# Convolution lags 0-15 by Karatsuba over pairs of token blocks, x and y in one buffer, and one filter strip of three loaded whole

## The chip, the cores and the metric

The kernel runs on one core of one Trainium2 chip. The metric is the device time of a run in microseconds. The four runs of the kernel before lie within 0.3% (2352.9 to 2360.5 us). Where a kernel was timed in rounds against the kernel before, the text gives the median and the ratio with its 95% interval; the other experiments are single runs with a profile. Profiles come from the hardware profiler on that core.

## The reference, cut to what matters

A causal convolution along the sequence, one filter per channel, is followed by a mixing layer, which the change does not touch.

```
x: (8, 5696, 128) float32        # batch, tokens, channels
h: (5696, 128) float32
y = irfft(rfft(x, n=2*S, axis=1) * rfft(h, n=2*S, axis=0), n=2*S, axis=1)[:, :S, :]
out = mixing_layer(y)            # two 5696 x 5696 products and more, 1765 us of the kernel before
```

## The kernel before: the parts that matter

Tokens are cut into 45 blocks of 128. For a channel d and a lag of k blocks, the filter gives a 128 x 128 Toeplitz matrix (each of its diagonals holds one value), and the matmul of lag k multiplies it with the first 45 - k blocks of x (8 batches each), so it has 8 x (45 - k) columns. The 45 matmuls of a channel accumulate into half of a tile in PSUM, the memory that matmuls write; the copy of a finished result out of it is called its eviction.

A Toeplitz matrix for all lags is a "strip": partition p holds the padded filter from place p on. A strip of 15 lags is read from memory into 64 partitions only (each row starts 2 bytes later than the row before). The other 64 partitions need the same data 64 places on, and VectorE copies them. Which half is loaded, and from which queue, alternates.

```python
x_sb = xsb_pool.tile([P, D, NT, B], BF16)                  # x, channel outermost
y_sb = ysb_pool.tile([P, NT, B, D], BF16)
...
with tc.tile_pool(name="conv_sbuf", bufs=6) as csb, ... :
    for d in range(D):
        ...
        for k0 in range(0, NT, KS):                        # KS = 15: three strips per channel
            strip = csb.tile([P, KS * P + 64], BF16, tag="strip")
            n_ = d * 3 + k0 // KS
            own, other, c0, c1 = ((slice(0, 64), slice(64, P), 0, 64) if n_ % 2 == 0 else
                                  (slice(64, P), slice(0, 64), 64, 0))
            eng = nc.sync if n_ % 2 == 0 else nc.scalar
            eng.dma_start(strip[own, :w + 64], ...)        # [[1, 64], [1, w + 64]] of h_pad
            nc.vector.tensor_copy(strip[other, c0:c0 + w], strip[own, c1:c1 + w])      # L158
            for k in range(k0, k1):                                                   # L162
                nc.tensor.matmul(psum[:, B * k: B * k + B * ntj], strip[:, c:c + P],
                                 x_sb2[:, d, :B * ntj], start=(k == 0), stop=(k == NT - 1))
        if d % 2 == 1:
            nc.scalar.activation(y_sb[...], pair[...], AF.Copy)                        # L167
```

## Time and profile before

The median is 2358.3 us of 4 runs (2352.9 to 2360.5).

| stage of the profiled run (2352.5 us) | us |
|---|---|
| filter and x loads, until the first matmul of the convolution | 108.1 |
| convolution, L162 | 479.8 |
| mixing layer | 1764.7 |

The first line below is part 1 of the page of the kernel before: each engine's busy time, its share of the span, and its number of instructions.

```profile
PE 2191.6 (93%) x14686; PEld 1210.8 (51%) x14686; DVE 1650.1 (70%) x2997; ACT 462.6 (20%) x669; POOL 798.2 (34%) x1474
```

A share over the whole span mixes stages with different limits. The next lines are the windows view of the same kernel for three stretches inside the convolution. Each line has the stretch, its length, busy us and instructions of PE (TensorE), PEld (its weight loads), DVE (VectorE), ACT (ScalarE) and POOL, then the granted clock, the DMA engines' mean busy share and the GB/s they moved.

```profile
core 0: us, PE busy (x) PEld busy (x) DVE busy (x) ACT busy (x) POOL busy (x), PEclk, DMA share, GB/s
200.00:300.00 100.00, 98.75 (x1206) 84.66 (x1203) 53.19 (x82) 11.13 (x14) 0.00 (x0) 1.00 0.74 207
300.00:400.00 100.00, 98.25 (x1204) 83.80 (x1202) 51.66 (x80) 10.31 (x13) 0.00 (x0) 1.00 0.73 206
400.00:500.00 100.00, 98.86 (x1211) 84.32 (x1210) 53.34 (x82) 11.13 (x14) 0.00 (x0) 1.00 0.73 206
```

TensorE is busy for 98 to 99% of the stage, VectorE for half of it, ScalarE for a tenth, and the DMA engines are not full. So TensorE sets the time of this stage.

From the groups of the page before: line, engine, operation, out<-in, shapes and number; then busy us and mean ns of one; then the engine's idle time in front of them and what ended it.

```profile
L162 PE MATMUL pair<-x_sb,strip 128*128 128x360 bf16 (+44 forms) x5760 | 472.0, 243 | 8.9 <-DVE strip L158 7.0
L158 DVE COPY strip<-strip 64x1920 bf16<-64x1920 bf16 x384 | 251.5, 655 | 228.1 <-DMA strip<-h_pad 194.8
```

The mean of 243 ns is a matmul's latency, not its cost: matmuls overlap (5760 of 243 ns would be 1400 us, in a stage of 480). The cost is the distance from one start to the next, which is in the trace: 152 ns for 360 columns, 99 for 232, 79 for 184, 56 for 128, and 25 for 40 columns and fewer. A line fitted to these, N/2.4 + 2.4 ns, meets the trace's medians from 360 down to 72 columns within 1.1 ns; no distance is under 25.

From part 6 of the same page, the DMA issues of the strips: queue, number, KB each, and the median us from issue to landing.

```profile
strip<-h_pad SPq DMA_DIRECT2D x192, 248.0 KB, 4.3
strip<-h_pad ACTq DMA_DIRECT2D x192, 248.0 KB, 4.3
```

### The profile page before, as it was taken

What the parts mean: (1) busy time and instruction counts of PE and PEld (TensorE: products, weight loads), DVE (VectorE), ACT (ScalarE), POOL (GpSimd) and SP (SyncE); (2) the same over time, 40 slices, a digit from 0 to 9 for tenths busy, and PEclk for the clock granted to TensorE, in tenths of its full rate; (3) what the DMA queues carried; (4) which work ended last, traced back from release to release, by engine and by line L of the source; (5) the groups of instructions that cost most, each with busy time, mean ns of one, the idle gap of its engine ahead of it and who ended that gap; (6) DMA issues with size and microseconds to landing.
All of it is one profiled execution on the core that took longest, in us unless ns stands there. A gap on an engine that the chain in (4) does not pass through costs nothing.

```text
span 2352.5 us, 39824 instructions
## 1 busy us (share of the span) xinstructions
PE 2191.6 (93%) x14686; PEld 1210.8 (51%) x14686; DVE 1650.1 (70%) x2997; ACT 462.6 (20%) x669; POOL 798.2 (34%) x1474
## 2 busy tenths in 40 slices
PE   4699999999657999999999999799999999999997
PEld 1188888888433444444444444334444444444443
DVE  5655555555668888887787677787777677677674
ACT  3411111110842332332322000001111111111111
POOL 0000000000211554554446654344454444544540
PEclk8599999999978999999999999999999999999998
DMA  9977777776997988998789997967887877977872
GB/s 240 251 208 205 206 203 207 207 205 192 261 293 192 162 165 162 166 167 152 139 163 167 156 151 131 291 107 130 146 144 134 153 140 131 156 133 136 152 133 56
DMA packets 435330, 405.50 MB, mean 172 GB/s; under 512 B 66496, under 2 KB 370624, under 8 KB 435008
## 3 DMA queue, kind: packets, MB, share of 16 engines
q0 software_dynamic: 222816, 131.33, 42.8%
q1 hardware_dynamic: 193936, 211.78, 30.6%
q10 hardware_dynamic: 18384, 59.85, 8.7%
q8 instruction: 116, 1.90, 0.3%
q14 instruction: 78, 0.64, 0.1%
HBM read 449.27 MB, written 84.75 MB: 227 GB/s over the span
## 4 chain that ended last, share of the span: by engine, by line
PE 77%; DMA 13%; DVE 6%; issue 2%; ACT 1%; SPq 1%; POOL 1%; DVEq 0%; ACTq 0%; POOLq 0%
PE m L604 56%; PE pair L162 15%; DMA strip<-h_pad 4%; DMA tmp<-in_x_dram 2%; DMA wb<-in_moe_w_tok_r_dram 2%; DVE c L611 1%; DMA b<-zi_hbm 1%; DMA h_bf<-in_h_dram 1%; PE v L425 1%; PE utp L418 1%; PE m L566 1%; PE m L568 1%; PE m L608 1%; DMA wb<-in_moe_w_tok_i_dram 1%; DVE wt L341 1%
## 5 line engine op out<-in xcount | busy, mean ns | idle before, releaser
L332 POOL DMA_DIRECT2D wb<-in_moe_w_tok_i_dram x720 | 390.6, 555 | 796.4 <-DVE wt L341 709.9
L332 POOL DMA_DIRECT2D wb<-in_moe_w_tok_r_dram x720 | 389.2, 557 | 704.5 <-PE pair L162 584.1
L162 PE MATMUL pair<-x_sb,strip 128*128 128x360 bf16 (+44 forms) x5760 | 472.0, 243 | 8.9 <-DVE strip L158 7.0
L604 PE MATMUL m<-b,wt 128*128 128x512 bf16 x1936 | 454.8, 381 | 18.7 <-ACT red L224 8.0
L162 PEld LDWEIGHTS <-strip 128*128 128x128 bf16 x5760 | 404.0, 98 | 77.6 <-DVE strip L158 12.9
L341 DVE STREAM_TRANSPOSE wt<-wb 128x384 f32<-128x384 f32 (+2 forms) x720 | 359.2, 522 | 119.9 <-PE m L604 72.0
L158 DVE COPY strip<-strip 64x1920 bf16<-64x1920 bf16 x384 | 251.5, 655 | 228.1 <-DMA strip<-h_pad 194.8
L604 PEld LDWEIGHTS <-wt 128*128 128x128 bf16 x1936 | 190.0, 98 | 252.1 <-issue 23.5
L611 DVE TENSOR_TENSOR c<-c,m 128x512 f32<-128x512 f32 x440 | 283.0, 668 | 0.0
L420 ACT ACTIVATE uts<-utp 128x512 bf16<-128x512 bf16 (+1 forms) x90 | 53.3, 592 | 614.4 <-PE utp L418 614.4
L167 ACT ACTIVATE y_sb<-pair 128x720 bf16<-128x720 f32 x64 | 50.9, 795 | 429.8 <-PE pair L162 368.1
L415 ACT ACTIVATE ub<-c 128x512 bf16<-128x512 f32 (+1 forms) x90 | 56.5, 628 | 224.6 <-DVE c L611 224.4
L121 PE MATMUL rps<-tmpbf,R_bf 128*128 128x512 bf16 x90 | 46.2, 616 | 51.0 <-DVE tmpbf L118 50.8
L118 DVE CAST tmpbf<-tmp 128x1024 bf16<-128x1024 f32 x45 | 56.4, 1261 | 32.4 <-DMA tmp<-in_x_dram 32.2
L191 ACT ACTIVATE yT<-tpz 128x512 bf16<-128x512 bf16 x68 | 39.7, 596 | 191.3 <-PE tpz L187 149.6
L427 DVE SCALAR_TENSOR_TENSOR c<-v,c 128x512 f32<-128x512 f32 (+1 forms) x90 | 61.4, 682 | 10.9 <-PE v L425 10.4
L205 ACT ACTIVATE red<-theta_ps,magic 128x512 f32<-128x512 f32 x46 | 31.6, 687 | 150.9 <-PE theta_ps L203 127.5
L225 ACT ACTIVATE mag<-mag,half_pi 128x512 f32<-128x512 f32 (+1 forms) x68 | 57.8, 851 | 0.2
L123 ACT ACTIVATE x_sb<-rps 128x1024 bf16<-128x1024 f32 x45 | 46.1, 1024 | 57.5 <-PE rps L121 57.2
L611 DVE TENSOR_TENSOR c<-yy,m 128x512 f32<-128x512 bf16 x88 | 56.0, 677 | 0.9 <-PE m L604 0.9
L121 PEld LDWEIGHTS <-R_bf 128*128 128x128 bf16 x90 | 6.2, 111 | 88.9 <-DVE tmpbf L118 80.1
L223 ACT ACTIVATE mag<-red 128x512 f32<-128x512 f32 x46 | 29.0, 630 | 78.0 <-DVE red L207 78.0
(2759 smaller groups left out, 2977.3 us busy)
## 6 DMA issues: line engine op xcount, KB each, us to landing
strip<-h_pad SPq DMA_DIRECT2D x192, 248.0 KB, 4.3
strip<-h_pad ACTq DMA_DIRECT2D x192, 248.0 KB, 4.3
wb<-in_moe_w_tok_r_dram POOLq DMA_DIRECT2D x352, 96.0 KB, 4.4
wb<-in_moe_w_tok_i_dram POOLq DMA_DIRECT2D x352, 96.0 KB, 4.8
wb<-in_moe_w_tok_r_dram POOLq DMA_DIRECT2D x352, 80.0 KB, 4.5
wb<-in_moe_w_tok_i_dram POOLq DMA_DIRECT2D x352, 80.0 KB, 3.7
tmp<-in_x_dram SPq DMA_DIRECT2D x44, 512.0 KB, 5.8
cp_hbm<-c SPq DMA_DIRECT2D x88, 256.0 KB, 2.4
```

Source lines behind the costliest of these rows:

```text
L118: nc.vector.tensor_copy(tmpbf, tmp.transpose([0, 2, 1]))
L121: nc.tensor.matmul(rps[:, h2 * 64:(h2 + 1) * 64, :], R_bf, tmpbf[:, h2 * 64:(h2 + 1) * 64, :], start=True, stop=True)
L158: nc.vector.tensor_copy(strip[other, c0:c0 + w], strip[own, c1:c1 + w])
L162: nc.tensor.matmul(psum[:, B * k: B * k + B * ntj], strip[:, c:c + P], x_sb2[:, d, :B * ntj], start=(k == 0), stop=(k == NT - 1))
L225: nc.scalar.activation(mag, mag, AF.Sin, bias=half_pi, scale=-TWO_PI)
L332: nc.gpsimd.dma_start(wb[32 * i:32 * i + 32, :ng, :nj * 64], bass.AP(tensor=a.tensor, offset=a.offset + row0 * S + p * H + i * QR + j0 * 6 ...
L341: nc.vector.transpose(wt.rearrange("p j t r -> p (j t r)").bitcast(F32).rearrange("p (j g t) -> p g j t", j=TJ, g=4)[:, :ng, :nj], wb[:, : ...
L415: nc.scalar.activation(ub[:m].rearrange("p b d -> p (b d)"), c[:m], AF.Copy)
L420: nc.scalar.activation(uts[:, :, :m], utp[:, :, :m], AF.Copy)
L427: nc.vector.scalar_tensor_tensor(c[:m], v[:m], 0.0, c[:m], op0=ALU.max, op1=ALU.add)
L604: nc.tensor.matmul(ms[q], a[q][:, j, :, r], bts[jj][q][:, r, :], start=(jj == 0 and r == 0), stop=(jj == NJ - 1 and r == 1 and q not in left))
L611: nc.vector.tensor_tensor(c, z, ms[q], op=op)
```

## The change

The intent is to take work from TensorE. Lags 0 to 15 couple token blocks in pairs (even and odd blocks), and three products of half length replace four (Karatsuba's scheme): the common term is taken once, from the difference of an even and an odd block of x, and the sums of neighbouring lags of the filter make the other two. That costs VectorE two sums and a difference per pair of channels, and an eviction with an addition in place of a plain copy. To pay for it, ScalarE takes over the copy of one strip, and the third strip is loaded into all 128 partitions, so that it needs no copy. x and y share one buffer, with channels innermost; each pair's x is copied out of it. All strips are issued from one queue (SyncE).

```diff
-    x_sb = xsb_pool.tile([P, D, NT, B], BF16)
+    xy = xy_pool.tile([P, NT + 1, B, D], BF16)
+    y_sb = xy[:, :NT, :, :]
...
+    LAGS = ((0, 2 * KX, 64), (2 * KX, 31, 64), (31, NT, 0))          # KX = 8
+    with tc.tile_pool(name="conv_strip", bufs=4) as csb, tc.tile_pool(name="conv_x", bufs=3) as cxb, ...
+        def conv_strips(d):
+            for n_, (k0, k1, halo) in enumerate(LAGS):
+                src = h_pad.offset + d * HW + P * k0
+                if halo == 0:                                         # the whole strip
+                    nc.sync.dma_start(strip, bass.AP(..., offset=src, ap=[[1, P], [1, w]]))
+                    continue
+                lower = (d + n_) % 2 == 0                             # own: 0-63 or 64-127
+                nc.sync.dma_start(strip[own, :], bass.AP(..., ap=[[1, 64], [1, w + 64]]))
+                if n_ == 0:
+                    nc.vector.tensor_copy(strip[other, ...], strip[own, ...])             # L156
+                else:
+                    nc.scalar.activation(strip[other, ...], strip[own, ...], AF.Copy)     # L158
+            nc.vector.tensor_add(q_, s0_[:, c0:c0 + w], s0_[:, c0 + P:c0 + P + w])        # L163
+        def conv_prepare(d):                                          # a pair of channels
+            nc.scalar.activation(xp..., xy[:, :, :, d:d + 2]..., AF.Copy)                 # L171
+            strips = [conv_strips(d + e) for e in range(2)]
+            nc.vector.tensor_sub(vd..., xp[:, :, 0, :, :]..., xp[:, :, 1, :, :]...)       # L175
+        nxt = conv_prepare(0)
+        for d in range(0, D, 2):
+            xp, vd, strips = nxt
+            nxt = conv_prepare(d + 2)                                 # one pair ahead
+            for e in range(2):
+                for k in range(KX):                                   # 24 products, L196-L200
+                    matmul(c_, b_, vd); matmul(odd blocks, q_, xp even); matmul(even blocks, q_, xp odd)
+                matmul(...)                                           # one of 120 columns, L203
+                for k in range(2 * KX, NT):                           # lags 16-44 as before, L209
+                    matmul(r, strip, xt)
+            nc.scalar.activation(c_sb..., c_ps..., AF.Copy)                               # L213
+            nc.vector.tensor_tensor(y of even blocks, rv[:, 0], cv, op=add)               # L217
+            nc.vector.tensor_tensor(y of odd blocks, rv[:, 1], cv, op=ALU.subtract)       # L218
```

More of the change, by code (lines that the diff above doesn't have):

```diff
@@ L40 @@
     HW = Sp + P
-    KS = 15
-    assert NT % KS == 0
     BD = B * D
@@ L74 @@
     ysb_ctx = ExitStack()
-    xsb_ctx = ExitStack()
-    xsb_pool = xsb_ctx.enter_context(tc.tile_pool(name="xsb", bufs=1))
-    x_sb = xsb_pool.tile([P, D, NT, B], BF16)
-    with tc.tile_pool(name="s0", bufs=1, side="right") as s0, \
-         tc.tile_pool(name="xload", bufs=4, side="right") as xl, \
+    xy_pool = ysb_ctx.enter_context(tc.tile_pool(name="xy", bufs=1, side="right"))
+    xy = xy_pool.tile([P, NT + 1, B, D], BF16)
+    y_sb = xy[:, :NT, :, :]
+    nc.vector.memset(xy[:, NT, :, :], 0.0)
+    with tc.tile_pool(name="s0", bufs=1) as s0, \
+         tc.tile_pool(name="xload", bufs=4) as xl, \
          tc.tile_pool(name="xlp", bufs=2, space=bass.MemoryType.PSUM) as xlp, \
@@ L116 @@
                                       ap=[[D, q_cnt], [S * D, B], [1, D]]))
-            tmpbf = xl.tile([P, D, B], BF16, tag="xbf")
-            nc.vector.tensor_copy(tmpbf, tmp.transpose([0, 2, 1]))
-            rps = xlp.tile([P, D, B], F32, tag="rps")
+            tmpbf = xl.tile([P, B * D], BF16, tag="xbf")
+            nc.vector.tensor_copy(tmpbf, tmp.rearrange("p b d -> p (b d)"))
+            rps = xlp.tile([P, B * D], F32, tag="rps")
             for h2 in range(2):
-                nc.tensor.matmul(rps[:, h2 * 64:(h2 + 1) * 64, :], R_bf,
-                                 tmpbf[:, h2 * 64:(h2 + 1) * 64, :], start=True, stop=True)
-            nc.scalar.activation(x_sb[:, :, tj, :], rps, AF.Copy)
+                nc.tensor.matmul(rps[:, h2 * 512:(h2 + 1) * 512], R_bf,
+                                 tmpbf[:, h2 * 512:(h2 + 1) * 512], start=True, stop=True)
+            nc.scalar.activation(xy[:, tj, :, :].rearrange("q b d -> q (b d)"), rps, AF.Copy)
         t = s0.tile([P, P], F32, tag="wt1")
@@ L130 @@
         nc.vector.tensor_copy(w_ch_sb, t)
-    ysb_pool = ysb_ctx.enter_context(tc.tile_pool(name="ysb", bufs=1, side="right"))
-    y_sb = ysb_pool.tile([P, NT, B, D], BF16)
-    x_sb2 = x_sb.rearrange("q d t b -> q d (t b)")
-    with tc.tile_pool(name="conv_sbuf", bufs=6) as csb, \
-         tc.tile_pool(name="conv_psum", bufs=2, space=bass.MemoryType.PSUM) as cps:
-        for d in range(D):
-            if d % 2 == 0:
-                pair = cps.tile([P, 2, 512], F32, tag="convps")
-            psum = pair[:, d % 2, :NT * B]
-            for k0 in range(0, NT, KS):
-                k1 = k0 + KS
-                w = KS * P
-                j0 = P * k0
-                strip = csb.tile([P, KS * P + 64], BF16, tag="strip")
-                n_ = d * 3 + k0 // KS
-                own, other, c0, c1 = ((slice(0, 64), slice(64, P), 0, 64) if n_ % 2 == 0 else
-                                      (slice(64, P), slice(0, 64), 64, 0))
-                eng = nc.sync if n_ % 2 == 0 else nc.scalar
-                eng.dma_start(strip[own, :w + 64],
-                              bass.AP(tensor=h_pad.tensor, offset=h_pad.offset + d * HW + j0,
-                                      ap=[[1, 64], [1, w + 64]]))
-                nc.vector.tensor_copy(strip[other, c0:c0 + w], strip[own, c1:c1 + w])
-                for k in range(k0, k1):
-                    ntj = NT - k
-                    c = c0 + (k - k0) * P
-                    nc.tensor.matmul(psum[:, B * k: B * k + B * ntj],
-                                     strip[:, c:c + P],
-                                     x_sb2[:, d, :B * ntj],
-                                     start=(k == 0), stop=(k == NT - 1))
-            if d % 2 == 1:
-                nc.scalar.activation(
-                    y_sb[:, :, :, d - 1:d + 1].rearrange("q t b e -> q (t b) e"),
-                    pair[:, :, :NT * B].rearrange("q e n -> q n e"), AF.Copy)
@@ L170 @@
-    xsb_ctx.close()
+    KX = 8
+    NJ2 = (NT + 1) // 2
+    assert NT == 2 * NJ2 - 1
+    LAGS = ((0, 2 * KX, 64), (2 * KX, 31, 64), (31, NT, 0))
+    with tc.tile_pool(name="conv_strip", bufs=4) as csb, \
+         tc.tile_pool(name="conv_x", bufs=3) as cxb, \
+         tc.tile_pool(name="conv_psum", bufs=2, space=bass.MemoryType.PSUM) as cps:
+        def conv_strips(d):
+            out_ = []
+            for n_, (k0, k1, halo) in enumerate(LAGS):
+                w = (k1 - k0) * P
+                strip = csb.tile([P, w + halo], BF16, tag=f"strip{n_}", name=f"strip{n_}")
+                src = h_pad.offset + d * HW + P * k0
+                if halo == 0:
+                    nc.sync.dma_start(strip, bass.AP(tensor=h_pad.tensor, offset=src,
+                                                     ap=[[1, P], [1, w]]))
+                    out_.append((strip, 0, k0))
+                    continue
+                lower = (d + n_) % 2 == 0
+                own, other, c0, c1 = ((slice(0, 64), slice(64, P), 0, 64) if lower else
+                                      (slice(64, P), slice(0, 64), 64, 0))
+                nc.sync.dma_start(strip[own, :],
+                                  bass.AP(tensor=h_pad.tensor, offset=src,
+                                          ap=[[1, 64], [1, w + 64]]))
+                if n_ == 0:
+                    nc.vector.tensor_copy(strip[other, c0:c0 + w], strip[own, c1:c1 + w])
+                else:
+                    nc.scalar.activation(strip[other, c0:c0 + w], strip[own, c1:c1 + w], AF.Copy)
+                out_.append((strip, c0, k0))
+            s0_, c0, _ = out_[0]
+            w = (2 * KX - 1) * P
+            q_ = csb.tile([P, w], BF16, tag="stripq", name="stripq")
+            nc.vector.tensor_add(q_, s0_[:, c0:c0 + w], s0_[:, c0 + P:c0 + P + w])
+            return out_, q_
+        def conv_prepare(d):
+            if d >= D:
+                return None
+            xp = cxb.tile([P, NJ2, 2, B, 2], BF16, tag="xp", name="xp")
+            nc.scalar.activation(xp.rearrange("q j p b e -> q (j p b) e"),
+                                 xy[:, :, :, d:d + 2].rearrange("q t b e -> q (t b) e"), AF.Copy)
+            strips = [conv_strips(d + e) for e in range(2)]
+            vd = cxb.tile([P, NJ2, B, 2], BF16, tag="vd", name="vd")
+            nc.vector.tensor_sub(vd.rearrange("q j b e -> q j (b e)"),
+                                 xp[:, :, 0, :, :].rearrange("q j b e -> q j (b e)"),
+                                 xp[:, :, 1, :, :].rearrange("q j b e -> q j (b e)"))
+            return xp, vd, strips
+        nxt = conv_prepare(0)
+        for d in range(0, D, 2):
+            xp, vd, strips = nxt
+            nxt = conv_prepare(d + 2)
+            r_ps = cps.tile([P, 2, 512], F32, tag="rps", name="r_ps")
+            c_ps = cps.tile([P, 2, 256], F32, tag="cps", name="c_ps")
+            for e in range(2):
+                (s0_, s1_, s2_), q_ = strips[e]
+                r = r_ps[:, e, :NT * B]
+                rj = r_ps[:, e, :2 * NJ2 * B].rearrange("q (j p b) -> q j p b", p=2, b=B)
+                c_ = c_ps[:, e, :NJ2 * B]
+                xt = xp.rearrange("q j p b e -> q (j p b) e")
+                strip, c0, _ = s0_
+                for k in range(KX):
+                    n = NJ2 - k
+                    b_ = strip[:, c0 + 2 * k * P:c0 + (2 * k + 1) * P]
+                    nc.tensor.matmul(c_[:, B * k:], b_, vd[:, :n, :, e],
+                                     start=(k == 0), stop=(k == KX - 1))
+                    nc.tensor.matmul(rj[:, k:NJ2 - 1, 1, :], q_[:, 2 * k * P:(2 * k + 1) * P],
+                                     xp[:, :n - 1, 0, :, e], start=(k == 0), stop=False)
+                    nc.tensor.matmul(rj[:, k:, 0, :],
+                                     q_[:, (2 * k - 1) * P:2 * k * P] if k else b_,
+                                     xp[:, :n, 1, :, e], start=False, stop=False)
+                nc.tensor.matmul(rj[:, KX:, 0, :], strip[:, c0 + (2 * KX - 1) * P:c0 + 2 * KX * P],
+                                 xp[:, :NJ2 - KX, 1, :, e], start=False, stop=False)
+                for strip, c0, k0 in (s1_, s2_):
+                    k1 = LAGS[1][1] if strip is s1_[0] else NT
+                    for k in range(k0, k1):
+                        c = c0 + (k - k0) * P
+                        nc.tensor.matmul(r[:, B * k:B * NT], strip[:, c:c + P],
+                                         xt[:, :B * (NT - k), e], start=False, stop=(k == NT - 1))
+            rv = r_ps[:, :, :2 * NJ2 * B].rearrange("q e (j p b) -> q p j b e", p=2, b=B)
+            c_sb = cxb.tile([P, NJ2, B, 2], F32, tag="csb", name="c_sb")
+            nc.scalar.activation(c_sb.rearrange("q j b e -> q (j b) e"),
+                                 c_ps[:, :, :NJ2 * B].rearrange("q e n -> q n e"), AF.Copy)
+            cv = c_sb
+            yv = xy[:, :, :, d:d + 2].rearrange("q (j p) b e -> q p j b e", p=2)
+            nc.vector.tensor_tensor(yv[:, 0], rv[:, 0], cv, op=add)
+            nc.vector.tensor_tensor(yv[:, 1, :NJ2 - 1], rv[:, 1, :NJ2 - 1], cv[:, :NJ2 - 1],
+                                    op=ALU.subtract)
```

## The prediction

> **What bounds the kernel now.** The change touches only the convolution. By line L162 its 5760 matmuls run from 108.1 to 587.7 us, 480 of 2352.5 us. TensorE bounds this stage: the windows 200-500 us show it 98 to 99% busy, VectorE 52%, ScalarE 11%, DMA share 0.73 at 206 GB/s. From the trace, one matmul follows the other after N/2.4 + 2.4 ns for N columns, never under 25 ns (360 columns 152 ns, 184 columns 79 ns, up to 40 columns 25 ns; strip boundaries excepted). A channel's 45 matmuls are then 3.62 us, 464 us for 128; the other 16 us are the half clock until 122.6 us and short waits for strips (20 us in the line view).
>
> **What changes on TensorE.** Lags 0-15 cost 4800 columns per channel, 2.04 us; Karatsuba does them with 24 half-length products and one of 120 columns, 3800 in all, so 1.64 us. Lags 16-44 stay at 1.59 us. That is 3.23 us per channel, 413 us for 128: 50 us less. This holds if strided operands (every second bf16; sums in runs of 8 floats) stream at the same rate; no matmul of this trace shows it.
>
> **What is added, per pair of channels (6.46 us of TensorE).** VectorE: two copies of half a strip (0.655 us for 1920 columns now, about 0.7 for 2048); two bf16 sums of 1920 columns (1024 take 0.68 us, 768 take 0.56, so 1.15 each); the difference, 0.4; two eviction sums of 368 and 352 floats (512 take 0.67, so 0.52): about 5.2 us. ScalarE: two half copies of 1920 (1024 elements take 1.02, so 1.8 each), the pair's x 0.83, the eviction 0.45: about 4.9 us. Both fit, VectorE at 80%, in a loop (eviction of a pair, then preparing the next but one) with little slack.
>
> DMA: a channel's strips grow from 762 to 983 KB because one is loaded whole, so 300 GB/s is wanted against 206. The page loads x at 287 and the products' operands at 360 GB/s; but half strips landing behind each other at the start came every 1.17 us, 217 GB/s. [...] If half strips do not overlap, 1.25 + 1.17 + about 1.15 = 3.6 us per channel, which would bind; overlapped, 3.0. I expect mostly overlap: 3.3 us.
>
> **Ends of the stage.** Strips can no longer be loaded during the x loads (their memory is what those loads use), and halves, sums and differences precede the first matmul: about +7 us. Last eviction +1. The x cast without transpose is cheaper, but x loading is bound by its DMA (tiles every 1.8 us): 0 to -2.
>
> **Sum.** 3.3 x 128 = 422, +7 half clock, +7 start, +1, a few us of waits: about 441 against 480. The rest is unchanged. Prediction **2321 us**, 2300 to 2352 eight times in ten. Faster by over 2% (under 2312) 0.34, within 2% 0.62, slower 0.04.
>
> **In the profile.** L162's successors: 54 matmuls per channel, 6912; stage about 440 us; same spacing per column; VectorE 75 to 85% there, ScalarE about 75%; DMA near 290 GB/s; first matmul near 114 us.
>
> **What would make it wrong.** Strided operands streaming slower; the strips' DMA binding at 3.6 us (then about 2355, TensorE waiting on strips); the VectorE loop longer than TensorE's 6.46 us; or less waiting than thought, which gives 2305.

422 + 7 + 7 + 1 and a few us of waits came to about 441 us for the stage, and 2321 in all. The 217 GB/s is the trace's (248 KB every 1.17 us); the 1.15 us of a whole strip and the 3.0 us of a channel with overlap were estimates, not shown by the trace (for the whole strip, the 377 GB/s of its window 1480 to 1485 us, a high one, would make it 1.22). The half clock until 122.6 us is not in the trace either: the granted clock is 0.50 from 108.1 to 112.0 us and 1.00 from there to 130.

## The result

The changed kernel takes 2432.4 us (median of 4 runs, 2427.8 to 2436.5) against 2358.3 us, both correct. The ratio is 1.032, with an interval of 1.029 to 1.035: slower by 3.2%. A ratio here is the mean time of one kernel's fast runs over that of the other's in the same rounds, so not quite the ratio of the medians quoted.

| stage of the profiled run | before | after |
|---|---|---|
| until the first matmul of the convolution | 108.1 | 111.0 |
| convolution | 479.8 | 549.3 |
| mixing layer | 1764.7 | 1765.7 |
| span | 2352.5 | 2426.1 |

The whole loss is in the convolution: 69.6 of 73.5 us, with 2.9 us more in front of it. Part 1 of the page after:

```profile
PE 2167.8 (89%) x15665; PEld 1237.5 (51%) x15838; DVE 1684.1 (69%) x3062; ACT 728.1 (30%) x861; POOL 796.7 (33%) x1474
```

The windows view after, same stretches and columns as before:

```profile
200.00:300.00 100.00, 82.74 (x1244) 77.73 (x1242) 54.74 (x79) 56.73 (x46) 0.00 (x0) 0.98 1.04 231
300.00:400.00 100.00, 84.22 (x1291) 78.93 (x1289) 58.07 (x84) 59.52 (x48) 0.00 (x0) 1.00 1.04 238
400.00:500.00 100.00, 84.17 (x1300) 80.73 (x1298) 58.07 (x84) 59.46 (x48) 0.00 (x0) 0.98 1.03 237
```

TensorE is no longer the limit (83 to 84%), and neither are VectorE and ScalarE (below 60%). The DMA engines' share has gone from 0.73 to 1.04, which is full: 231 to 238 GB/s. A channel's strips are 983,040 bytes (64 x 4224 + 64 x 3968 + 128 x 3584), so 4.15 us per channel at the 237 GB/s of the last window. 128 of them are 531 us of the stage's 549; from 120 to 200 us the rate was lower, 215 to 217 GB/s.

The strips' issues after, from part 6 of the page; the first line is the whole strips:

```profile
strip<-h_pad SPq DMA_DIRECT2D x128, 448.0 KB, 11.5
strip<-h_pad SPq DMA_DIRECT2D x128, 264.0 KB, 11.4
strip<-h_pad SPq DMA_DIRECT2D x128, 248.0 KB, 10.7
```

A strip now lands about 11 us after its issue, against 4.3 before: the loads stand in a queue. Who waited for whom between 200 and 500 us, after (us in total, times, longest; the first four lines of the answer):

```profile
DVE strip L156 <- DMA strip<-h_pad: 113.9, 68, 4.0
ACT strip L158 <- DMA strip<-h_pad: 66.2, 39, 3.0
ACT xp L171 <- PE r_ps L209: 55.1, 35, 2.3
PEld L198 <- DVE stripq L163: 52.9, 54, 1.4
```

The copies wait for strips, and TensorE waits for what is made from the copies. The third line is of another kind: ScalarE's copy of a pair's x waits for matmuls, though it is meant for a pair that has not begun. It becomes important below.

The new instructions cost what they were estimated at (groups of the page after):

```profile
L158 ACT ACTIVATE strip<-strip 64x1920 bf16<-64x1920 bf16 x128 | 230.7, 1802 | 133.4 <-DMA strip<-h_pad 129.7
L156 DVE COPY strip<-strip 64x2048 bf16<-64x2048 bf16 x128 | 88.2, 689 | 214.3 <-DMA strip<-h_pad 214.1
L163 DVE TENSOR_TENSOR stripq<-strip 128x1920 bf16<-128x1920 bf16 x128 | 147.5, 1153 | 2.2
L171 ACT ACTIVATE xp<-xy 128x736 bf16<-128x736 bf16 x64 | 55.4, 869 | 96.2 <-PE r_ps L209 96.1
```

And the matmuls' spacing barely suffers from the strided operands: 56 ns for 128 columns with the products into runs of 8 floats (56 before), 103 ns for 232 columns with every second bf16 (99 before).

So two questions were open: why the DMA engines, full, move only 237 GB/s when slices of the same page further on show 285 and 305, and whether the DMA is the only limit.

### The profile page after: what moved, and what is told of

Read it like the earlier page. It is cut to its first block, busy times and chain, and to the rows that moved or that the text cites. A ratio compares the mean times of both kernels' runs of the same rounds, so it can differ in the third digit from the quotient of the medians.

```text
span 2426.1 us, 42014 instructions
## 1 busy us (share of the span) xinstructions
PE 2167.8 (89%) x15665; PEld 1237.5 (51%) x15838; DVE 1684.1 (69%) x3062; ACT 728.1 (30%) x861; POOL 796.7 (33%) x1474
## 4 chain that ended last, share of the span: by engine, by line
PE 61%; DMA 24%; DVE 8%; issue 2%; ACT 2%; POOL 2%; SPq 1%; DVEq 0%; ACTq 0%; another core or an unknown queue 0%; POOLq 0%
PE m L653 50%; DMA strip<-h_pad 15%; PE r_ps L209 2%; DVE c L660 2%; DMA wb<-in_moe_w_tok_i_dram 2%; DMA tmp<-in_x_dram 2%; POOL wb L381 1%; DMA b<-zi_hbm 1%; DMA wb<-in_moe_w_tok_r_dram 1%; DMA h_bf<-in_h_dram 1%; DVE stripq L163 1%; PE r_ps L198 1%; PE utp L467 1%; PE v L474 1%; DVE wt L390 1%
## 5 line engine op out<-in xcount | busy, mean ns | idle before, releaser
L158 ACT ACTIVATE strip<-strip 64x1920 bf16<-64x1920 bf16 x128 | 230.7, 1802 | 133.4 <-DMA strip<-h_pad 129.7
L156 DVE COPY strip<-strip 64x2048 bf16<-64x2048 bf16 x128 | 88.2, 689 | 214.3 <-DMA strip<-h_pad 214.1
L209 PE MATMUL r_ps<-xp,strip 128*128 128x232 bf16 (+28 forms) x3712 | 228.9, 216 | 1.4 <-ACT strip L158 1.1
L198 PE MATMUL r_ps<-xp,stripq 128*128 128x176 bf16 (+7 forms) x1024 | 153.9, 229 | 78.4 <-DVE stripq L163 77.7
L209 PEld LDWEIGHTS <-strip 128*128 128x128 bf16 x3712 | 220.4, 96 | 5.2 <-ACT strip L158 2.1
L163 DVE TENSOR_TENSOR stripq<-strip 128x1920 bf16<-128x1920 bf16 x128 | 147.5, 1153 | 2.2
L198 PEld LDWEIGHTS <-stripq 128*128 128x128 bf16 x1024 | 98.8, 97 | 96.9 <-DVE stripq L163 96.2
L200 PE MATMUL r_ps<-xp,stripq 128*128 128x176 bf16 (+6 forms) x896 | 130.1, 229 | 0.0
L196 PE MATMUL c_ps<-vd,strip 128*128 128x184 bf16 (+7 forms) x1024 | 93.3, 232 | 19.8 <-DVE strip L156 18.9
L200 PEld LDWEIGHTS <-stripq 128*128 128x128 bf16 x896 | 86.5, 96 | 0.0
L171 ACT ACTIVATE xp<-xy 128x736 bf16<-128x736 bf16 x64 | 55.4, 869 | 96.2 <-PE r_ps L209 96.1
L196 PEld LDWEIGHTS <-strip 128*128 128x128 bf16 x1024 | 71.8, 96 | 24.1 <-DVE strip L156 23.4
```

The costliest lines, as they stand in the source:

```text
L158: nc.scalar.activation(strip[other, c0:c0 + w], strip[own, c1:c1 + w], AF.Copy)
L163: nc.vector.tensor_add(q_, s0_[:, c0:c0 + w], s0_[:, c0 + P:c0 + P + w])
L196: nc.tensor.matmul(c_[:, B * k:], b_, vd[:, :n, :, e], start=(k == 0), stop=(k == KX - 1))
L198: nc.tensor.matmul(rj[:, k:NJ2 - 1, 1, :], q_[:, 2 * k * P:(2 * k + 1) * P], xp[:, :n - 1, 0, :, e], start=(k == 0), stop=False)
L200: nc.tensor.matmul(rj[:, k:, 0, :], q_[:, (2 * k - 1) * P:2 * k * P] if k else b_, xp[:, :n, 1, :, e], start=False, stop=False)
L209: nc.tensor.matmul(r[:, B * k:B * NT], strip[:, c:c + P], xt[:, :B * (NT - k), e], start=False, stop=(k == NT - 1))
```

## The experiments

The theories, by the letters that the expectations use:

- **S**: the source. All DMA engines read the same 4 KB of memory in overlapping rows.
- **A**: rows start at any even byte, unaligned.
- **Q**: one queue cannot keep the DMA engines busy.
- **P**: the destination. The 64 partitions that a half strip is written to, 0-63 or 64-127, make it slow, and with it what stands in the same queue.
- **C**: contention of the DMA with the compute engines at the on-chip memory.
- **D**: the engines move any strip at no more than some 240 GB/s.
- **O**: not the DMA but the order of the engines' instructions sets the time.

Stage times below run from the first to the last matmul of the convolution. Kernels marked "wrong" give a wrong result.

### 1 to 3. Rows apart, rows apart but unaligned, all rows the same (wrong)

```diff
-                src = h_pad.offset + d * HW + P * k0
+                src = h_pad.offset + P * k0               # e1, e2; e3 keeps the old line
-                         ap=[[1, P], [1, w]]     and     ap=[[1, 64], [1, w + 64]]
+                         ap=[[HW, P], [1, w]]    and     ap=[[HW, 64], [1, w + 64]]     # e1
+                         HW + 1 in place of HW                                          # e2
+                         0 in place of 1                                                # e3
```

> Wrong result on purpose: partition p of each strip reads row p of the padded filter (a row is 11776 bytes) instead of a place 2 bytes after partition p-1; same bytes, same destinations, same queue. After the change the strips' DMA is saturated: 237 GB/s, a strip lands 11 us after its issue, a whole one takes 1.95 us and a half one 1.15 us. Theory S (the source: all 16 DMA engines read the same 4 KB of memory at once, in rows that overlap) says that rows lying apart are read faster: stage from 549 to 440 to 470 us, total about 2320 to 2350, whole strips 1.2 us. Theory A (rows that start at any even byte) says the same here. Theory P (the destination side or a general limit near 240 GB/s) says no change: total within 15 us of 2432. Theory Q (one queue for all strips) says no change either.

> Wrong result on purpose: as e1_apart, but every row starts 2 bytes later in its own row, so rows lie apart and start unaligned as in the changed kernel. Theory S (overlap): fast like e1_apart, 2320 to 2350. Theory A (unaligned starts): slow like the changed kernel, about 2432. P and Q: about 2432.

> Wrong result on purpose: all partitions of a strip read the same aligned row, so the overlap is complete and every start aligned. Theory S: as slow as the changed kernel or slower, 2432 or more. Theory A: fast, 2320 to 2350. P and Q: about 2432.

Measured: 2429.5, 2429.7 and 2441.6 us. With rows apart and aligned, the stage took 551.3 us, the DMA 230 to 238 GB/s, and strips landed 11.6 us after their issue. Between 200 and 500 us the traces' packets give 235, 236 and 228 GB/s for the three runs, against 235 in the changed kernel. S and A fall as the cause: rows apart, aligned or not, leave the rate where it was. With all rows the same it is 3% lower and the stage 562 us, so the source is not without effect, but that effect is small here.

### 4. The whole strips from another queue

```diff
-                    nc.sync.dma_start(strip, bass.AP(tensor=h_pad.tensor, ...
+                    nc.scalar.dma_start(strip, bass.AP(tensor=h_pad.tensor, ...
```

> Right result: the whole strip of each channel is issued from ScalarE's queue, the half ones from SyncE's. Theory Q (one queue cannot keep the DMA engines busy): DMA rate rises from 237 GB/s, total under 2400. Theories S, A and P: total within 15 us of 2432, landing still near 11 us.

Measured: 2439.8 us, correct. The landing times fell to 8 to 10 us, but the rate did not rise (229 GB/s between 200 and 500 us, from the trace's packets). Q falls.

### 5. Twelve patterns of loads, with the compute engines idle

Between the x loads and the convolution, groups of 12 loads were put on the queue behind each other, each group into the same 12 tiles.

```diff
+    PATS = [[(ALL, 1792, 1, SY)], [(LO, 2112, 1, SY)], ..., [(MID, 2112, 1, SY)], ...]   # rows, columns, step, queue
+    for n, pats in enumerate(PATS):                      # simplified here
+        for i in range(12):
+            rows, w_, stride, eng = pats[i % len(pats)]
+            eng.dma_start(tile_i[rows, :w_], bass.AP(tensor=h_pad.tensor, ..., ap=[[stride, rows.stop - rows.start], [1, w_]]))
```

> Right result; a measurement beside the kernel. Between the x loads and the convolution, while the compute engines are idle, twelve groups of 12 strip loads run behind each other on the queue: 1 whole strips of 3584-byte rows, 2 half strips into partitions 0-63 only, 3 half strips into 0-63 and 64-127 in turn, 4 the changed kernel's mix of half, half, whole, 5 whole with rows that lie behind each other in memory, 6 whole with 4096-byte rows, 7 the same with rows behind each other, 8 whole with rows 11776 bytes apart, 9 half strips into partitions 32-95, 10 whole from two queues, 11 whole with all rows the same, 12 whole with 2048-byte rows. Theory P[...]: group 2 near 217 GB/s, group 9 near 350, groups 1 and 5 to 8 near 350, group 4 between. Theory C (what binds is contention with the compute engines at the on-chip memory): all groups but 2 run at 300 GB/s or more here, group 4 too, and only with the matmuls running 237. Theory D (the DMA engines move any strip at no more than about 240 GB/s): groups 1 to 8 all near 240. Total: 2432 plus 200 to 280 us for the groups.

Measured: 2657.5 us, correct. The windows view of this run, for the stretch from the third to the eleventh landing of groups 1 (whole strips), 2 (half strips into partitions 0-63), 3 (lower and upper in turn), 4 (lower, upper, whole) and 9 (half strips into partitions 32-95); the last column is GB/s:

```profile
113.40:126.70 13.30, 0.00 (x0) 0.00 (x0) 0.00 (x0) 0.00 (x0) 0.00 (x0) 0.50 0.92 276
134.70:145.40 10.70, 0.00 (x0) 0.00 (x0) 0.00 (x0) 0.00 (x0) 0.00 (x0) 0.50 1.01 195
153.50:162.10 8.60, 0.00 (x0) 0.00 (x0) 0.00 (x0) 0.00 (x0) 0.00 (x0) 0.50 0.91 215
169.10:178.50 9.40, 0.00 (x0) 0.00 (x0) 0.00 (x0) 0.00 (x0) 0.00 (x0) 0.50 1.03 273
...
261.70:267.70 6.00, 0.00 (x0) 0.00 (x0) 0.00 (x0) 0.00 (x0) 0.00 (x0) 0.50 0.98 361
```

The same 64 rows of 4224 bytes move at 195 GB/s into partitions 0-63 and at 361 GB/s into 32-95. Theory P had expected near 217 and near 350. So the partitions that are written decide here; by what mechanism, the runs do not show. D falls too: rows behind each other in memory ran at 401 GB/s. What did not fit was the mix, at 273 GB/s against 237 in the kernel. In group 1, all twelve loads read one channel's filter (276 GB/s); with rows 11776 bytes apart the same loads ran at 363. So the source can matter: theory P had groups 1 and 6 near 350, and they ran at 276 and 299, while 5, 7 and 8 (rows not overlapping) ran at 401, 412 and 363. In the kernel it hardly did (runs 1 to 3).

### 6 and 7. Few matmuls; no strip copies (wrong)

```diff
-                for k in range(KX):                        # e6
+                for k in (0,):
-                    for k in range(k0, k1):
+                    for k in (k0, k1 - 1):
```

In e7 the strips lie in fixed tiles that are cleared once, and the two copies are left out.

> Wrong result on purpose: 8 of a channel's 54 matmuls are left, all loads, copies and sums stay. TensorE would need about 80 us for the stage. If the strips' DMA binds by itself (theories P and D), the stage stays at 540 to 555 us and the DMA rate at 235 to 240 GB/s; if matmuls slow the DMA (theory C, TensorE's part), the rate rises and the stage falls towards VectorE's 5.3 us per pair, 340 to 400 us.

> Wrong result on purpose: the strips lie in fixed buffers cleared once, and the copies from the loaded half to the other half are left out, on VectorE and ScalarE; loads, sums, matmuls and evictions stay. Theory C (the copies' traffic at the on-chip memory slows the DMA from the 273 GB/s of the quiet mix to 237): the DMA rate rises to 260 GB/s or more, the stage from 549 to 500 us or less. Theory P (half strips[...], in a queue with whole ones): rate 235 to 245, stage 530 to 550.

Measured: 2409.2 us and a stage of 529.6 us with 8 of 54 matmuls; 2435.3 us and 552.6 us without copies. One of the windows of e6:

```profile
300.00:400.00 100.00, 34.68 (x201) 20.19 (x200) 61.00 (x86) 60.31 (x50) 0.00 (x0) 1.00 1.04 242
```

With six matmuls of seven gone, TensorE is busy for a third of the time and the stage is 20 us shorter; the DMA is as full as before, at 239 to 243 GB/s (226 to 241 without copies). Both stages just miss the ranges that P expected (540 to 555, 530 to 550). This answers what TensorE's saving of 50 us could be worth in the changed kernel: next to nothing, since taking away far more of its work brought 20 us. C falls as the cause of the rate: with few matmuls it is at most 3% higher, and without copies no higher.

### 8. Half strips into partitions 32-95 (wrong)

The fixed tiles of e7, and

```diff
-                nc.sync.dma_start(strip[own, :],
+                nc.sync.dma_start(strip[32:96, :],
-                    nc.vector.tensor_copy(strip[other, c0:c0 + w], strip[own, c1:c1 + w])     # likewise on ScalarE
+                    nc.vector.tensor_copy(strip[0:32, c0:c0 + w], strip[64:96, c1:c1 + w])
```

> Wrong result on purpose: the strips lie in fixed buffers cleared once, and each half strip is loaded into partitions 32 to 95 in place of 0 to 63 or 64 to 127[...]; bytes, queue, sources, matmuls stay, each copy handles 32 partitions with as many columns as before and so takes as long. Theory P: the half strips' landing interval falls from 1.1 to 0.75 us as in the quiet measurement (360 GB/s), DMA 280 GB/s or more, stage 430 to 480 us. If the DMA stays near 237 GB/s and the stage at 530 or more, P falls too.

Measured: 2467.5 us, stage 590.4 us: slower, although the DMA did what P says. Part 6 of the page of this run, then one of its windows:

```profile
strip<-h_pad SPq DMA_DIRECT2D x128, 448.0 KB, 4.1
strip<-h_pad SPq DMA_DIRECT2D x128, 264.0 KB, 3.5
strip<-h_pad SPq DMA_DIRECT2D x128, 248.0 KB, 3.1
```

```profile
300.00:400.00 100.00, 75.13 (x1163) 71.15 (x1161) 53.90 (x77) 53.08 (x44) 0.00 (x0) 1.00 0.64 216
```

Strips land in 3 to 4 us in place of 11, and the DMA is only 0.64 busy. Nothing is full in this run, and yet it is slower than the changed kernel. So in this kernel there is another limit, which is not an engine's or the DMA's throughput. The expected stage, 430 to 480 us, was missed because of it. The copies of 32 partitions do take as long as those of 64, as was expected: the mean instruction of this window is 1.21 us on ScalarE and 0.70 on VectorE, against 1.24 and 0.69 in the changed kernel's.

### 9. All three strips by half (correct)

```diff
-    LAGS = ((0, 2 * KX, 64), (2 * KX, 31, 64), (31, NT, 0))
+    LAGS = ((0, 2 * KX, 64), (2 * KX, 31, 64), (31, NT, 64))
-                lower = (d + n_) % 2 == 0
+                lower = (d * 3 + n_) % 2 == 0
-                if n_ == 0:                                # VectorE copies strips 0 and 2
+                if n_ != 1:
```

> Right result: one part of the change undone. The third strip is again loaded by half, into the two halves of the partitions in turn, and VectorE copies the other half (0.62 us each). Bytes per channel fall from 983 to 766 KB. If the stage is bound by the bytes at some 237 GB/s: 3.2 us per channel, so TensorE and VectorE (6.5 us a pair) bind: stage 425 to 445 us, total 2305 to 2330. If half strips are bound[...] at 217 GB/s or less (theory P): 3.5 us, stage 450 to 460, total 2335 to 2345.

(The bytes per channel are 761,856, as before the change; the expectation's 766 KB is a slip.)

Measured: 2477.2 us, stage 596.8 us. Both expectations are missed: 22% fewer bytes and a longer stage, with the DMA at 164 GB/s and 0.59 busy. The second limit shows here in plain form. ScalarE's timeline over one pair of channels (start us, length, instruction, and in brackets its idle time before it and what ended that):

```profile
410.04 0.86 ACT L171 ACTIVATE xp<-xy 128x736 bf16<-128x736 bf16 x1 [1.88 <-PE r_ps L209]
410.92 1.80 ACT L158 ACTIVATE strip<-strip 64x1920 bf16<-64x1920 bf16 x1
415.18 0.48 ACT L213 ACTIVATE c_sb<-c_ps 128x368 f32<-128x368 f32 x1 [2.46 <-PE c_ps L196]
415.68 1.80 ACT L158 ACTIVATE strip<-strip 64x1920 bf16<-64x1920 bf16 x1
419.36 0.92 ACT L171 ACTIVATE xp<-xy 128x736 bf16<-128x736 bf16 x1 [1.88 <-PE r_ps L209]
```

and who waited in this run between 200 and 500 us (three of the five lines of the answer):

```profile
PEld L209 <- ACT strip L158: 87.6, 64, 1.5
ACT c_sb L213 <- PE c_ps L196: 81.0, 33, 2.5
ACT xp L171 <- PE r_ps L209: 60.1, 32, 1.9
```

TensorE waits for strip copies, and ScalarE, which makes them, waits for TensorE. The source writes ScalarE's work as: x copy of the next pair, its two strip copies, then the eviction of this pair. The compiled program has another order, as the trace shows: the written order of ScalarE's instructions is not kept here. Numbering the pairs in this trace, the x copy of pair 22 starts at 297.63 us, at the end of pair 19's matmuls, and the strip copies of pair **20**, whose matmuls began at 297.45, come behind it, at 298.52 and 303.28. The x copy had moved two pairs ahead. Its tile has three buffers, so it has to wait until pair 19 releases one, and the copies that pair 20 needs at once stand behind it in ScalarE's queue. The second strip copy stands behind the eviction of pair 20, which waits for pair 20's own matmuls. So the parts no longer overlap: x copy 0.88 us, strip copy 1.86, 29 matmuls and the products in front of the eviction 2.40, eviction 0.50, strip copy 1.86, 29 matmuls 1.82, counted from start to start, are the 9.32 us that a pair takes. The changed kernel has the first inversion too (in its trace, pair 22's x copy at 290.96, pair 20's matmuls from 291.13, its strip copies at 292.39 and 296.98), behind the full DMA. It does not have the second: its eviction comes behind both strip copies. ScalarE in the changed kernel:

```profile
409.45 0.85 ACT L171 ACTIVATE xp<-xy 128x736 bf16<-128x736 bf16 x1 [1.37 <-PE r_ps L209]
410.32 1.80 ACT L158 ACTIVATE strip<-strip 64x1920 bf16<-64x1920 bf16 x1
413.86 1.80 ACT L158 ACTIVATE strip<-strip 64x1920 bf16<-64x1920 bf16 x1 [1.73 <-DMA strip<-h_pad]
415.68 0.48 ACT L213 ACTIVATE c_sb<-c_ps 128x368 f32<-128x368 f32 x1
```

So the compile gave e9, and e8 likewise (9.2 us per pair, eviction between the strip copies), another ScalarE order than the change has. An edit made for an experiment changed two things at once, and e8 and e9 do not show what the changed kernel's own order would cost with the DMA relieved. An estimate from e9's trace: x copy 0.88 us, strip copy 1.86, the first channel's 29 matmuls and the second's products 3.32, the last 29 matmuls 1.82, so 7.9 us per pair and some 505 us for the stage. That is under the 549 us that the DMA takes and over the 430 that TensorE needs; no run shows it.

### 10 to 12. The order held

`tc.keep_in_program_order` pins an instruction behind the one written before it on its engine (e12's timeline below has the written order). It was put around every VectorE and ScalarE instruction of the convolution, in three kernels: the changed one, e8 and e9. TensorE's instructions were not held, and their order changed too: in e10 to e12 the products with the difference (c_ps) of a pair's first channel come behind that channel's other matmuls, where in the changed kernel, e8 and e9 they come first.

```diff
+        keep = tc.keep_in_program_order
-                    nc.scalar.activation(strip[other, c0:c0 + w], strip[own, c1:c1 + w], AF.Copy)
+                    keep(nc.scalar.activation(strip[other, c0:c0 + w], strip[own, c1:c1 + w], AF.Copy))
...                                                        # likewise the other seven
```

> Right result: the changed kernel with VectorE's and ScalarE's instructions of the convolution held in the order in which they are written; the compile had moved the x copy of a pair ahead of the strip copies of the pair two before it, so that it waits for a pair of matmuls to end with those copies behind it. Theory O (that order, not the DMA, sets the time): stage falls from 549 to 440 to 480 us. Theory P (the strips' DMA[...], binds whatever the order): stage 535 to 550, DMA near 240 GB/s.

> Wrong result on purpose: half strips loaded into partitions 32-95 as in e8_mid_ports (DMA unsaturated, stage 586 us), and the order held as in e10_in_order. If there are two bounds, DMA and order, both are gone: stage 415 to 450 us, total near 2310. If order was not what held e8_mid_ports, the stage stays near 586.

> Right result: all three strips by half as in e9_all_halves (stage 597 us, DMA 164 GB/s, 0.58 busy), and the order held. Theory O: the stage falls to 430 to 470 us, bound by half strips at about 215 GB/s (3.55 us per channel) or by VectorE (6.5 us a pair); total 2310 to 2350, faster than before or equal. If the order is not the cause: 2477 stays.

Measured:

| strips | order as compiled | order held |
|---|---|---|
| two by half, one whole (the change) | 2432.4 us, stage 549 | e10: 2424.1 us, stage 547 |
| half strips in partitions 32-95 | e8: 2467.5 us, stage 590 | e11: 2312.1 us, stage 430 |
| all by half | e9: 2477.2 us, stage 597 | e12: 2315.4 us, stage 429 |

e10 and e11 came out inside the ranges of theory P and of two bounds, e12's stage 1 us below its range. (e8's stage is 590 us; the 586 in e11's expectation is not what its trace gives.) One window each of e10, e11 and e12:

```profile
300.00:400.00 100.00, 82.88 (x1273) 80.43 (x1271) 58.62 (x83) 58.76 (x48) 0.00 (x0) 0.98 1.02 236
```

```profile
300.00:400.00 100.00, 100.00 (x1642) 99.66 (x1640) 74.76 (x107) 74.23 (x61) 0.00 (x0) 1.00 0.85 299
```

```profile
300.00:400.00 100.00, 99.74 (x1625) 99.28 (x1623) 90.17 (x136) 72.72 (x61) 0.00 (x0) 1.00 0.94 231
```

In the changed kernel the order held brings 8 us, one run against the median of four, which is the size of the noise: the DMA is still full at 236 GB/s. From e10 to e11, with the order held in both, the half strips go to other partitions (into fixed tiles, which in e7 left the DMA full), and the stage falls from 547 to 430 us. This is what the strips' DMA cost. From e8 to e11 and from e9 to e12, with the DMA relieved, holding the order takes the stage from 590 and 597 us to 430 and 429, with TensorE busy for 99 to 100% of the time. So there are two limits, and no kernel with only one of them removed gained anything clear. The second one is that of the order that e8 and e9 were compiled to. That it sits in ScalarE's order is argued from e9's timeline, whose parts add up to the pair's 9.32 us; no run held ScalarE alone.

ScalarE's timeline in e12 over one pair:

```profile
410.90 0.48 ACT L215 ACTIVATE c_sb<-c_ps 128x368 f32<-128x368 f32 x1
411.28 0.84 ACT L173 ACTIVATE xp<-xy 128x736 bf16<-128x736 bf16 x1
412.35 1.80 ACT L160 ACTIVATE strip<-strip 64x1920 bf16<-64x1920 bf16 x1 [0.23 <-DMA strip<-h_pad]
415.38 1.80 ACT L160 ACTIVATE strip<-strip 64x1920 bf16<-64x1920 bf16 x1 [1.23 <-DMA strip<-h_pad]
417.21 0.48 ACT L215 ACTIVATE c_sb<-c_ps 128x368 f32<-128x368 f32 x1
```

The x copy no longer waits for matmuls, and the strip copies are made for the pair that comes next. e12 is correct, and it was timed: 2315.4 us (median of 4 runs, 2311.1 to 2316.0) against 2357.2 us in the same rounds, ratio 0.982 with an interval of 0.981 to 0.984. It beats the kernel before by 1.8%, with the change's arithmetic kept.

### 13. The mixes of the kernels, with the compute engines idle

What stayed open was the rate itself: 237 GB/s in the kernel, 273 in run 5. Run 5's mix kept the order lower, upper, whole. The kernel alternates: lower, upper, whole, upper, lower, whole. Run 13 measured that, 36 loads for each group and 12 in flight as in the kernel, in front of e12's convolution.

```diff
+    PATS = [mix((LO, UP, ALL, UP, LO, ALL)), mix((LO, UP, ALL)), mix((MID, MID, ALL)),
+            mix((LO, UP, ALL, UP, LO, ALL), stride=HW), mix((LO, UP, LO, UP, LO, UP), ws=(2112, 1984, 1856)), ...]
```

> Right result; a measurement beside e12_halves_in_order. With the compute engines idle, eight groups of 36 strip loads, 12 in flight as in the kernels: 1 the changed kernel's own turn (lower half, upper half, whole, upper, lower, whole), 2 lower, upper, whole, 3 both halves into partitions 32-95, then whole, 4 like 1 with rows apart, 5 lower and upper in turn with the three sizes of e12, 6 the same from two queues, 7 like 3 with rows apart, 8 all whole with rows apart. [...]group 1 shows 230 to 245 here too, group 4 the same, group 3 near 300 and group 5 near 230. If group 1 stays at 270 or more, the kernel's 237 has a further cause in the running kernel, which stays open. Total: 2315 plus 380 to 480 us.

Measured: 2665.6 us, correct. The windows of groups 1 (the changed kernel's turn), 2 (lower, upper, whole), 3 (both halves into 32-95, then whole), 4 (like 1, with rows apart) and 5 (the halves of e12):

```profile
121.10:163.70 42.60, 0.00 (x0) 0.00 (x0) 0.00 (x0) 0.00 (x0) 0.00 (x0) 0.50 1.03 205
176.90:210.40 33.50, 0.00 (x0) 0.00 (x0) 0.00 (x0) 0.00 (x0) 0.00 (x0) 0.50 1.04 263
222.10:244.20 22.10, 0.00 (x0) 0.00 (x0) 0.00 (x0) 0.00 (x0) 0.00 (x0) 0.50 1.03 410
258.70:295.10 36.40, 0.00 (x0) 0.00 (x0) 0.00 (x0) 0.00 (x0) 0.00 (x0) 0.50 1.04 243
307.40:336.70 29.30, 0.00 (x0) 0.00 (x0) 0.00 (x0) 0.00 (x0) 0.00 (x0) 0.50 1.04 234
```

With every engine idle, the change's turn of strips moves 205 GB/s, less than in the kernel, and the same bytes from the same places with the halves in partitions 32-95 move 410. In group 1 a row of a whole strip (3584 bytes) takes its DMA engine 277 ns on average, in group 3 it takes 143: the whole strips, which go to all 128 partitions in both groups, are slowed by the halves around them, to nearly twice the time. So the destination partitions by themselves bring a low rate. They are not the only thing that acts: with rows 11776 bytes apart the same turn moves 243 GB/s (group 4), while halves in 32-95 with whole ones move 410 with rows apart too (group 7), and whole strips alone with rows apart 409 (group 8). Partitions take the rate from 410 to 243, overlapping rows from there to 205; in the kernel rows apart brought nothing (e1). Of the expected rates, group 5's came true; groups 1 and 3 were off (230 to 245 and near 300 expected, should the destination of the halves alone make the kernel's 237), and so was the statement that 4 is like 1. Why the alternating turn is worse than the fixed one (205 against 263), and why the running kernel, at 237, does a little better than the quiet group, was not settled. The halves of e12 from two queues (group 6) ran at 230 GB/s, against 234 from one. Lower and upper halves in turn moved 215 GB/s against 195 for lower ones alone within run 5 (groups 3 and 2), and 234 in run 13, so 10 to 20% more, and far from double.

## Why the prediction was wrong, point by point

- **What bounds the kernel before**: right. TensorE, 98 to 99% busy in the stage.
- **TensorE's work**: right in mechanism and size. 3.23 us per channel was predicted; e11, which TensorE bounds, ran 1636 matmuls in 100 us on average over its three windows, 54 per channel, so 3.30. Strided operands cost a few ns per matmul.
- **VectorE's and ScalarE's work per pair**: right. From the groups, VectorE 2 x 0.689 + 2 x 1.153 + 0.34 + 0.553 + 0.518 = 5.1 us (5.2 predicted), ScalarE 2 x 1.80 + 0.87 + 0.48 = 4.95 (4.9 predicted).
- **The strips' DMA**: this step failed. The text said "I expect mostly overlap: 3.3 us", with 3.6 us per channel as the bad case. Measured: 4.15 us (983,040 bytes at 237 GB/s). The rate of the half strips in that case, 217 GB/s, was near what run 5 shows for lower and upper in turn (215), but even the bad case let a whole strip run at full rate (1.15 us, an estimate) once its turn came. With the order held, moving the half strips to partitions 32-95 took the stage from 547 to 430 us (e10, e11). In the queue with half strips, a whole one came 1.95 us after the landing before it in the changed kernel (mean over the trace), and its rows take 249 ns each on a DMA engine, where they take 140 ns with the halves in partitions 32-95 (medians of the packets between 200 and 500 us, after and e8). So the term of the sum that was mis-sized is 128 x 3.3 = 422 us, which is 531.
- **The order of the instructions**: this was not in the prediction at all. It took each engine to run what is written, in the order written ("in a loop (eviction of a pair, then preparing the next but one)"). The trace of before could not show the order that the compile would choose for the new code. In the changed kernel this cost nothing that stands out of the noise (e10), since the DMA was full anyway, so it is not what failed the prediction. In e8 and e9, with the DMA relieved and another order compiled, it was the whole loss.
- **Ends of the stage**: the first matmul at 111.0 us, 114 predicted. The half clock was put at +7 us, with "the half clock until 122.6 us"; the trace of before has the full clock from 112.0 us on (its window 100 to 130 us shows 0.80), so some 2 us by estimate. This slip of 5 us made the prediction higher, not lower. The x cast is cheaper, as the text says: 0.69 us after, 1.26 before (the mean of 45).
- **The sum**: 2321 us was predicted; the changed kernel takes 2432, and the same arithmetic with both limits removed takes 2315. TensorE's gain is real and was not reachable with the strips loaded as the change loads them.

## What to carry to other kernels

When a change takes work from the bounding engine and pays in DMA bytes, cost the DMA for the partitions that it writes (in run 5 the same rows moved at 195 GB/s into 0-63 and at 361 into 32-95) and for the mix that stands in the queue, not by the rate that other loads of the kernel reach; a few dozen loads placed in an idle stretch of the kernel measure it in one run, roughly (205 GB/s in run 13, 237 in the kernel). After a change that adds small instructions to several engines, compare the compiled order with the written one, and in the trace ask for whose benefit each instruction runs: one that waits for matmuls in order to serve a pair two steps ahead holds up all that stands behind it. Any edit, that of an experiment too, can change the compiled order (e8, e9): compare the orders before comparing the times. Where there are two limits, an experiment that removes one can look like a failure: look which resource went idle before dropping the idea, and try the two together.
